# Attention on one Trainium2 core: output stores held back for nine pairs of quads instead of seven, in twelve buffers instead of ten, and a wait ahead of the last nine

## The chip, the cores and the metric

The kernel runs on one core of one Trainium2 chip. The metric is the device time of one execution in microseconds; the median of seven runs is compared. The engines of the core are named as the profile names them: PE is TensorE's matmuls and PEld its weight loads, DVE is VectorE, ACT is ScalarE, POOL is GpSimd, SP is SyncE. A DMA is issued from the queue of an engine, here SP's (listed as q1) or ACT's (q10), and is carried out by the 16 DMA engines that all queues share.

## The reference

Softmax attention without a mask, for 16 x 32 = 512 heads, each with 192 queries, 1024 keys and a head size of 128, all bfloat16:

```
B, H, Sq, Sk, D = 16, 32, 192, 1024, 128

def reference(q, k, v):
    scale = q.shape[-1] ** -0.5
    scores = jnp.einsum("bhqd,bhkd->bhqk", q, k) * scale
    p = _softmax(scores, axis=-1)
    return jnp.einsum("bhqk,bhkd->bhqd", p, v)
```

The inputs are normal numbers times 0.05. Per head, 0.27 MB of keys, as much of values and 0.05 MB of queries come in, and 0.05 MB of output goes out.

## The kernel before

**Quads, fills and pairs.** Four heads make a quad; there are NQ = 128 quads. The work of a quad is cut into three fills, so there are NF = 384 fills, numbered f. For a fill, PE computes scores (`qk`, line 655), ACT takes the exponential from PSUM to SBUF (lines 861 and 864), and PE multiplies with the values (`pv`, line 678) LAG = 4 fills later. The values carry a column of ones, so the same matmuls give the sums of the softmax; DVE takes their reciprocals and scales the result into an output buffer `ob` (`onorm`, line 777, with the reciprocal in line 784 and the scaling in line 788). PE runs `qk` and `pv` of six fills as the body of a loop (line 715), and the last fill and the last four `pv` as straight code behind it. Two quads make a pair; one store writes a pair, 384 KB.

**Ahead of the matmuls.** SP loads keys, queries and values of a quad (lines 558, 543 and 567) into five buffers each. DVE turns the keys (line 763) and queries (line 772), POOL puts the keys in order (line 620) and spreads the values (line 629). A load waits until its buffer is free: the keys until DVE has turned those of five quads ago, the values until `pv` has used those of five quads ago.

**Stores.** `stores` (line 452) lists 65 of them: 63 pairs, and the last two quads one by one. Store i takes buffer i modulo NSO, with NSO = 10, from `ob`. A store in the list `store_at` (line 539) is issued from ACT's queue, behind the exponentials of fill 3(x + c) + 6 + 6 HOLD, where x is its first quad and c the number of its quads. HOLD = 7 puts the store of the first pair behind fill 54, and one store follows every six fills. Only those that come out at fill 372 or before are in the list: 54 of them, numbers 0 to 53. The other eleven are issued by SP in the order of the list, behind its last load (line 596). Each waits until DVE has passed its quads (semaphore s_rc); the store of the last quad is two DMAs of 96 KB, each with a wait for its own `onorm` (s_fin). A DMA-issuing instruction of SP also stays as long as its queue takes no more.

**Buffers that come free.** `onorm` of a pair's first fill waits until the store that used the same buffer NSO pairs ago has landed (line 787).

**The end.** The `pv` of fills 380 to 382 write to the PSUM of scores, so that of fill 380 waits for the exponential before last, and that of fill 381 for the last exponential and the last spread values (lines 683 to 689). DVE then looks over all reciprocals and writes one number, `redo`, which says whether a general version of the kernel has to run; with these inputs it doesn't. Each engine reads `redo` behind a barrier, jumps over the general version and meets the others at a last barrier. SP waits there for all stores to land (`stored`, line 598).

Of the kernel before, what the change touches and what calls it, by code (L numbers as in the profile page):

```python
# [421 lines left out]
def _attention_kernel(nc, q, k, v, out):  # L422
# [9 lines left out]
    NF = 3 * NQ  # L432
    LAG = 4

    PRE = 1
# [3 lines left out]
    NKN, NVS, NKT, NVP = 5, 5, 2, 2  # L439
    GQ = 2  # L440

    NSO, HOLD = 10, 7

    HELD = 2
    VB = 136
# [9 lines left out]
    with ExitStack() as outer:  # L455
        redo = outer.enter_context(nc.sbuf_tensor("redo", [1, 1], mybir.dt.int32))

        def sem(name):
            return outer.enter_context(nc.semaphore(name))
# [13 lines left out]
        s_qk = sem("f_qk")  # L473
# [11 lines left out]
        with ExitStack() as es:  # L485
# [34 lines left out]
            def store(e, i):  # L520
                so = i % NSO
                x, c = stores[i]
                if x + c == NQ:

                    for y in range(2):
                        e.wait_ge(s_fin, y + 1)
                        e.dma_start(
                            of[4 * x + 2 * y:4 * x + 2 * y + 2].rearrange("x (p j) d -> (x p) (j d)", j=3),
                            ob[:, so, 3 * y:3 * y + 3, :].rearrange("p j d -> p (j d)"),
                        ).then_inc(s_st[so], 16)  # L530
                    return
                e.wait_ge(s_rc, 3 * (x + c) + 1)
                e.dma_start(
                    of[4 * x:4 * x + 4 * c].rearrange("(a x) (p j) d -> (x p) a (j d)", x=2, j=3),
                    ob[:, so, 0:6 * c, :].rearrange("p (a j) d -> p a (j d)", j=3),
                ).then_inc(s_st[so], 16)


            store_at = {3 * (x + c) + 6 + 6 * HOLD: i for i, (x, c) in enumerate(stores)
                        if 3 * (x + c) + 6 + 6 * HOLD <= NF - 12}  # L540

            def load_q(e, x):
                e.dma_start(
                    qn[:, x % NKN, :],
                    qf[4 * x:4 * x + 4].rearrange("a (j u) d -> (a j) (u d)", u=6).bitcast(U32),
                ).then_inc(s_qn[x % NKN], 16)
# [3 lines left out]
            def hint(eng):  # L550
                hints[eng.engine] = eng.mark_branch_hint_location()

            @block.sync
            def _(e):
                def load_k(x, lo=0, hi=32):
                    if x >= NKN:
                        e.wait_ge(s_kx, 3 * (x - NKN) + 3)
                    e.dma_start(
                        kn[:, x % NKN, 64 * lo:64 * hi],
                        kf[4 * x:4 * x + 4].rearrange("a (j r) d -> (a j) r d", r=32)[:, lo:hi, :]  # L560
                        .rearrange("p r d -> p (r d)").bitcast(U32),
                    ).then_inc(s_kn[x % NKN], 16)

                def load_v(x, lo=0, hi=4):
                    if x >= NVS:
                        e.wait_ge(s_pv, 3 * (x - NVS) + 2 + BLANK)
                    e.dma_start(
                        vs[:, x % NVS, lo:hi, :],
                        vf[4 * x + lo:4 * x + hi].rearrange("a (m t) d -> m a (t d)", t=T),
                    ).then_inc(s_v[x % NVS], 16)  # L570


                load_k(0)
                e.wait_ge(s_blank, 1)
                load_k(1)
                load_q(e, 1)
                load_v(0, 0, 2)
                e.wait_ge(s_qk, PRE + 1)
                load_v(0, 2, 4)
                load_k(2, 0, 16)  # L580
                e.wait_ge(s_pv, BLANK - 2)
                load_k(2, 16, 32)
                load_q(e, 2)
                for n in range(3, NKN):
                    load_v(n - 2)
                    load_k(n)
                    load_q(e, n)
                for n in range(NQ):
                    if n == NQ // 2:
                        hint(e)  # L590
                    if n + NKN - 2 < NQ:
                        load_v(n + NKN - 2)
                    if n + NKN < NQ:
                        load_k(n + NKN)
                        load_q(e, n + NKN)
                for i in range(len(store_at), len(stores)):
                    store(e, i)
            def stored(e):
                for so in range(NSO):
                    last = (len(stores) - 1) % NSO == so  # L600
                    e.wait_ge(s_st[so], 16 * (len(range(so, len(stores), NSO)) + last))
# [269 lines left out]
def bass_standalone__mha_softmax__near_ridge_kernel(  # L871
    nc: bass.Bass,
    q: bass.AP,
    k: bass.AP,
    v: bass.AP,
    out: bass.AP,
):
    _attention_kernel(nc, q, k, v, out)
# [28 lines left out]
```

## Time and profile before

| | us |
|---|---|
| Median of 7 runs | 815.38 (814.43 to 817.21) |
| The profiled execution, as timed | 816.05 |
| Its span, from the first to the last instruction | 814.3 |
| PE idle in the span | 14.1 |
| Median time of one fill on PE, `qk` and `pv` | 2.054 |
| Last score fill starts | 801.13 |
| Last `pv` ends | 808.9 |
| Last store issued | 809.6 |
| Last of DVE's work (`redo`) | 810.5 |

PE's instructions are busy for 98% of the span, ACT's for 92%, DVE's for 74% and POOL's for 68%. The core reads 293.60 MB and writes 25.17 MB. In the DMA rows, the share is the busy time of the 16 engines together; a share of 1.0 or a little more is full.

Three kinds of lines come below. A row of windows gives, for a stretch of time, its length and then for each engine the busy time with the number of instructions, then the clock that was granted to TensorE, the DMA share and the GB/s. A row of waits gives who waited for what, the total in us, how often, and the longest. A row of the chain of waits, or of the timeline, begins with the start in us and the length in us; in the timeline, the square bracket tells how long the engine was idle before, and what ended it.

### The profile page before, as it was taken

The page shows a single profiled execution, that of the slowest core. Times are in us where ns is not written, and L with a number is a line of the kernel's source. Part 1 is how long each engine was busy: PE and PEld are TensorE (multiplying, and loading weights), DVE is VectorE, ACT ScalarE, POOL GpSimd, SP SyncE. Part 2 cuts the span into 40 slices and gives each one's busy share as a digit, 9 for nine tenths or more (in the row PEclk, how much of TensorE's full clock was granted, in tenths as well). Part 3 has the DMA queues.
Part 4 walks back from the last instruction along what each step waited for, and adds up shares of the span by engine and source line. Part 5 has one row for each costly group of instructions (what it writes and reads, how often), then busy time and mean ns, then how long its engine had stood idle before and what let it go on. Part 6 is the DMA issues. An engine that isn't in the chain of part 4 may idle for free. (4 is left out here: it accounts for less than half of the span.)

```text
span 814.3 us, 71452 instructions
## 1 busy us (share of the span) xinstructions
PE 800.2 (98%) x32996; PEld 714.1 (88%) x32996; DVE 600.7 (74%) x1293; ACT 749.9 (92%) x772; POOL 552.2 (68%) x648
## 2 busy tenths in 40 slices
PE   7999999999999999999999999999999999999996
PEld 6888888888888888888888888888888888888885
DVE  4777777777777777777777777777777777778773
ACT  6899999999999999999999999999999999998994
POOL 5676676676677677667667667766676676766772
PEclk9999999999999999999999999999999999999999
DMA  7999999999999999999999999999999999999995
GB/s 259 405 397 403 399 401 403 409 404 405 409 404 406 408 405 405 407 405 405 408 405 405 407 405 405 405 404 398 398 378 396 402 405 406 381 409 404 385 367 167
DMA packets 138474, 319.20 MB, mean 392 GB/s; under 512 B 7232, under 2 KB 56384, under 8 KB 122176
## 3 DMA queue, kind: packets, MB, share of 16 engines
q1 hardware_dynamic: 109776, 297.36, 93.7%
q10 hardware_dynamic: 28656, 21.43, 7.8%
q14 instruction: 35, 0.29, 0.1%
q8 instruction: 7, 0.11, 0.1%
HBM read 293.60 MB, written 25.17 MB: 391 GB/s over the span
## 5 line engine op out<-in xcount | busy, mean ns | idle before, releaser
L864 ACT ACTIVATE f_pt<-f_s 128x1536 bf16<-128x1536 f32 x384 | 554.5, 1444 | 0.1
L699 PE MATMUL f_o<-f_vp,f_pt 128*64 128x129 bf16 x12368 | 425.4, 222 | 2.0 <-PEq L653 1.8
L670 PE MATMUL f_s<-f_qt,f_kt 32*128 32x192 bf16 (+1 forms) x20528 | 422.7, 226 | 4.2 <-PEq L653 3.4
L620 POOL COPY f_kt<-f_kx 128x768 uint32<-128x768 uint32 (+1 forms) x384 | 300.4, 789 | 185.4 <-DVE f_kx L763 184.4
L699 PEld LDWEIGHTS f_o<-f_vp,f_pt 128*64 128x64 bf16 x12368 | 362.3, 110 | 51.0 <-issue 24.2
L670 PEld LDWEIGHTS f_s<-f_qt,f_kt 32*128 32x128 bf16 x20528 | 348.8, 92 | 40.8 <-issue 5.4
L763 DVE STREAM_TRANSPOSE f_kx<-f_kn 128x768 uint32<-128x768 uint32 (+1 forms) x384 | 334.3, 871 | 27.0 <-DMA f_kn<-in_k_dram 23.6
L629 POOL COPY f_vp<-f_vs 128x1024 uint32<-128x1024 uint32 x256 | 259.9, 1045 | 63.1 <-DMA f_vs<-in_v_dram 62.3
L861 ACT ACTIVATE f_pt<-f_s 128x512 bf16<-128x512 f32 x384 | 229.3, 597 | 52.9 <-PE f_s L670 10.0
L784 DVE RECIPROCAL f_rinv<-f_o 128x2 f32<-128x2 f32 x381 | 64.5, 169 | 165.4 <-PE f_o L699 164.9
L788 DVE TENSOR_TENSOR f_ob<-f_o,f_rinv 128x256 bf16<-128x256 f32 x381 | 161.8, 425 | 13.0
L772 DVE STREAM_TRANSPOSE f_qt<-f_qn 128x384 uint32<-128x384 uint32 x128 | 72.9, 570 | 0.0
L699 PE MATMUL f_s<-f_vp,f_pt 128*64 128x129 bf16 x96 | 3.3, 220 | 1.6 <-issue 1.5
L699 PEld LDWEIGHTS f_s<-f_vp,f_pt 128*64 128x64 bf16 x96 | 2.9, 110 | 1.9 <-issue 1.7
L848 ACT ACTIVATE f_pt<-f_ones 128x1536 f32<-128x1536 bf16 x3 | 4.2, 1472 | 0.0
L608 POOL MEMSET f_vp<- 128x1088 uint32 (+1 forms) x3 | 3.8, 1311 | 0.0
L784 DVE RECIPROCAL f_rinv<-f_s 128x2 f32<-128x2 f32 x3 | 0.5, 170 | 2.6 <-PE f_s L699 2.6
L848 ACT ACT_TABLE_LOAD x1 | 1.3, 1283 | 1.2 <-PEq L892 1.2
L712 PE MATMUL f_o<-f_ones 128*128 128x512 bf16 x2 | 1.0, 622 | 1.1 <-POOL f_ones L605 1.1
L736 DVE MEMSET f_pt<- 128x256 uint32 x4 | 1.1, 272 | 0.9 <-PEq L892 0.9
L729 PE MATMUL f_o<-f_bad,f_ones 128*1 128x1 bf16 x1 | 0.2, 164 | 1.4 <-DVEq L837 1.4
L788 DVE TENSOR_TENSOR f_ob<-f_s,f_rinv 128x256 bf16<-128x256 f32 x3 | 1.3, 424 | 0.3 <-DVE f_rinv L784 0.3
(15 smaller groups left out, 5.6 us busy)
## 6 DMA issues: line engine op xcount, KB each, us to landing
f_kn<-in_k_dram SPq DMA_DIRECT2D x127, 1024.0 KB, 18.0
f_vs<-in_v_dram SPq DMA_DIRECT2D x127, 1024.0 KB, 16.2
f_qn<-in_q_dram SPq DMA_DIRECT2D x127, 192.0 KB, 14.2
out_dram<-f_ob ACTq DMA_DIRECT2D x54, 384.0 KB, 9.5
out_dram<-f_ob SPq DMA_DIRECT2D x9, 384.0 KB, 7.2
f_vs<-in_v_dram SPq DMA_DIRECT2D x2, 512.0 KB, 5.8
f_kn<-in_k_dram SPq DMA_DIRECT2D x2, 512.0 KB, 5.1
f_qn<-in_q_dram ACTq DMA_DIRECT2D x1, 192.0 KB, 5.7
```

The source lines that it names most:

```text
L608: return gp.memset(part.bitcast(U32), 0x3F803F80)
L620: gp.tensor_copy(kt[:, x % NKT].bitcast(U32).rearrange("p U (j s u) c -> p U j s (u c)", s=2, u=2)[:, lo:hi], kx[:, x % 2].rearrange("p (U ...
L629: gp.tensor_copy(vp[:, x % NVP, 2 * T * i: 2 * T * i + 2 * T, 0:D].bitcast(U32), vs[:, x % NVS, 2 * i: 2 * i + 2, :].rearrange("p a (t d) ...
L670: ins = pe.matmul(S[:, c0: c0 + n1 - n0], kt[r, x % NKT, 2 * t + h, :, c], qt[r, x % R, h, n0:n1, c], start=w == 0 and g == 0, stop=w == 3 ...
L699: ins = pe.matmul(O[64 * z: 64 * z + 64, u, 0:129], pt[:, x % R, 2 * y + z, t * SQ + 64 * j: t * SQ + 64 * j + 64], vp[:, x % NVP, (2 * y ...
L763: dve.transpose(kx[:, x % 2].rearrange("p (U s j u) -> p s u U j", s=2, j=32, u=2)[:, :, :, lo:hi], kn[:, x % NKN].rearrange("p (s u U i) ...
L772: dve.transpose(qt[:, x % R].bitcast(U32).rearrange("p b (y j u) c -> p u y b (j c)", y=3, u=2), qn[:, x % NKN].rearrange("p (u y b i) -> ...
L784: dve.reciprocal(ri, O[:, :, 128]).then_inc(s_rc, 1)
L788: ins = dve.tensor_tensor(ob[:, so, 6 * a + 2 * w: 6 * a + 2 * w + 2, :], O[:, :, 0:128], ri.unsqueeze(2).to_broadcast([128, 2, D]), ALU.mult,
L848: return act.activation(part.bitcast(F32), ones[:, 0:1].to_broadcast([128, 2 * T * SQ // 2]), ACT_FN.Copy)
L861: act.activation(pt[:, x % R, 0, c], s1_ps[:], ACT_FN.Exp, scale=scale).then_inc(s_e1, 1)
L864: act.activation(pt[:, x % R, 1:4, c], s3_ps[f % 2][:], ACT_FN.Exp, scale=scale).then_inc(s_e3, 1)
```

## The change

NSO goes from 10 to 12 and HOLD from 7 to 9. The first store then stands behind fill 66, and 52 stores (numbers 0 to 51) are in ACT's list, so SP issues thirteen behind its last load. It issues four of them, numbers 52 to 55; ahead of the fifth, number 56, it waits until all 385 score fills are counted (s_qk of NF + PRE, where PRE = 1 counts one blank fill at the start). `ob` grows by two buffers of 3 KB in each partition, and `stored` waits for twelve semaphores instead of ten.

```diff
@@ -439,7 +439,7 @@
     NKN, NVS, NKT, NVP = 5, 5, 2, 2
     GQ = 2
 
-    NSO, HOLD = 10, 7
+    NSO, HOLD = 12, 9
 
     HELD = 2
     VB = 136
@@ -594,6 +594,9 @@
                         load_k(n + NKN)
                         load_q(e, n + NKN)
                 for i in range(len(store_at), len(stores)):
+
+                    if i == len(store_at) + 4:
+                        e.wait_ge(s_qk, NF + PRE)
                     store(e, i)
             def stored(e):
                 for so in range(NSO):
```

## The prediction

> **What bounds the kernel now.** I read the busy times first, then windows of 40 us, the waits, and the last 15 us piece by piece.
>
> ```profile
> PE 800.2 (98%) x32996; PEld 714.1 (88%) x32996; DVE 600.7 (74%) x1293; ACT 749.9 (92%) x772; POOL 552.2 (68%) x648
> ```
>
> PE is busy nearly throughout, so only its 14.1 us of idle time can be won, and what lies behind its end. The windows tell where the idle time is:
>
> ```profile
> 80.00:120.00 40.00, 40.00 (x1673) 35.80 (x1671) 29.93 (x66) 37.81 (x40) 27.15 (x33) 1.00 1.04 400
> 200.00:240.00 40.00, 40.00 (x1678) 35.73 (x1668) 30.40 (x66) 37.71 (x40) 28.48 (x34) 1.00 1.04 404
> 640.00:680.00 40.00, 40.00 (x1652) 35.84 (x1648) 30.61 (x65) 37.70 (x41) 28.92 (x34) 1.00 1.04 407
> 680.00:720.00 40.00, 39.51 (x1642) 35.13 (x1637) 29.38 (x64) 36.93 (x39) 26.48 (x31) 1.00 1.03 394
> 720.00:760.00 40.00, 39.16 (x1622) 34.91 (x1622) 32.05 (x67) 36.80 (x39) 28.08 (x32) 1.00 1.03 396
> ```
>
> PE has no gap until 680 us and loses 0.49 and 0.84 us in the two rows after. By the starts of the score fills the loss is larger: those between 684 and 766 us stand 2.03 us further apart, in sum, than at the 2.054 us per fill of all others. The DMA share is 1.03 or 1.04 in every row, before the first store (125.1 us) as well as behind it: the DMA engines are always full. The waits say who is late:
>
> ```profile
> POOL f_vp L629 <- DMA f_vs<-in_v_dram: 12.8, 12, 2.1
> ...
> POOL f_vp L629 <- DMA f_vs<-in_v_dram: 16.2, 9, 2.2
> ```
>
> ```profile
> 745.92 2.03 POOL L629 COPY f_vp<-f_vs 128x1024 uint32<-128x1024 uint32 x2 [2.21 <-DMA f_vs<-in_v_dram]
> ...
> 749.71 0.52 PE L670 MATMUL f_s<-f_qt,f_kt 32*128 32x64 bf16 x22 [0.72 <-PEq L653]
> ```
>
> These are the windows 540 to 640 and 640 to 690 us; from 140 to 540 us POOL never waits for values. At 745.92 the spreading starts 2.21 us late, the ordering of keys behind it on POOL is late too, and PE stands still for 0.72 us. So the loads have a lead that they lose. By the landing records, values land 0.7 us ahead of their spreading in quad 8 (63.8 and 64.5 us), 4.15 us in quad 16 (109.6 and 113.8), 4.6 us in quad 26 (170.8 and 175.4) and 0.05 us from quad 90 (569.6) on. One of the 16 engines drops behind the others: keys of quad 16 land between 98.8 and 100.7 us, of quad 96 between 588.2 and 597.0. The lead is its lead.
>
> The last stretch is another matter:
>
> ```profile
> 802.27 0.60 ACT f_pt L861
> 802.87 1.35 ACTq L485
> 804.22 0.04 issue
> 804.26 0.24 PE f_s L699
> 804.50 1.52 issue
> 806.02 1.97 PE f_s L699 x63
> ```
>
> ```profile
> 802.00:803.00 1.00, 1.00 (x42) 0.85 (x32) 0.00 (x0) 0.89 (x3) 0.00 (x0) 1.00 1.03 319
> 803.00:804.00 1.00, 1.00 (x42) 0.99 (x36) 0.60 (x2) 1.00 (x1) 0.00 (x0) 1.00 1.06 333
> 804.00:805.00 1.00, 0.40 (x7) 0.11 (x2) 0.59 (x2) 0.21 (x1) 0.00 (x0) 1.00 0.69 217
> 805.00:806.00 1.00, 0.00 (x0) 0.00 (x0) 0.00 (x0) 0.00 (x0) 0.00 (x0) 1.00 0.14 45
> ```
>
> Behind the last exponential PE loads two sets of weights and stops for 1.52 us with no semaphore to wait for. The DMA list shows what comes in meanwhile: one packet of the queue of instructions that feeds PE,
>
> ```profile
> q8 instruction: 1, 0.02, 11.8%
> ```
>
> at 803.58 us, for 0.95 us. Such packets are seen only in the first 25 us and behind PE's loop. Until 804.3 us the engines are full of SP's stores (319 to 333 GB/s).
>
> **The change part by part.** *Two stores leave the stretch before the last load.* With HOLD = 9, 52 instead of 54 stores are issued from ACT's queue ahead of it; they start 12 fills, 24.6 us, later. What two stores cost the loads has three prices. By bytes at 404 GB/s: 2 x 393,216 B / 404 GB/s = 1.95 us. By the lead: it grew 0.435 us a quad without stores (quads 8 to 16: 3.48 us / 8) and 0.05 with them (quads 20 to 26), 0.77 us for a store of two quads, 1.54 for two. The third is what is left if the loads couldn't use the stretch without stores, being held by full buffers: then the loss only starts 24.6 us later, and 2.03 us over 122 us (from 684 - 16 to 790) is 1.66%, 0.41 us. Against the third speaks the share of 1.04 before 125 us. PE's loss is what the last loads are late, so it shrinks by as much, to at least 0: I take 1.75 us, the middle of the first two, with 0.41 and 2.03 as ends. The last score fill ends at 802.25 - 1.75 = 800.50.
>
> *Four stores behind the last load, then the wait.* In the stretch around 800 us there is no store traffic but of those four, on the engine that is behind. So the instruction packet can start earlier. The next one, at 807.11 with the engines idle (share 0.08), started 1.09 us after PE had gone on at 806.02. The stall of 1.52 us is worth between 0 and 1.52 us; a packet that meets the stores' burst could make it longer. I take 1.52, as the stores are the only other traffic.
>
> Here the page "Runtime: NRT & Kernel Launch" of the Trainium skill, section "Instruction fetch mechanics", speaks against the price: instructions come in blocks of 16 KiB while the block before runs, and the cost of crossing into the next one is mostly hidden. The 1.52 us above are not hidden; by the rule the term would be 0.
>
> *Nine stores behind the wait.* SP is free when the last score fill is counted, as ACT is at 802.27, now 800.52. Queued behind the wait on SP are seven stores of 384 KB, one of 192 KB and the two halves. How fast do they go?
>
> ```profile
> L533 SPq DMA_DIRECT2D out_dram<-f_ob x4: 829/1076/1203, 798.0 to 801.4; - x4
> ...
> DMA to landing us min/median/max: 5.7/6.0/6.2
> ```
>
> ```profile
> L527 SPq DMA_DIRECT2D out_dram<-f_ob x2: 344/344/345, 808.7 to 809.6; - x2
> ```
>
> With the engines full of stores alone they move 320 GB/s (799 to 803 us), 1.23 us for 384 KB. The last half, issued at 809.60, had its first packet at 810.44, 0.84 later, its last at 810.84 and landed at 811.23, 0.39 later. So: 800.52 + 0.84 + 8 x 1.23 (the small ones make one more) + 0.39 = 811.59. From the landing SP needs 0.7 us: its other waits and its drain, 0.35 (812.38 to 812.91 for all of them before, most of it still to come), then the barrier, 814.0 to 814.3. End: 812.3.
>
> *The other way to the end*, by PE, DVE, the barrier and ACT's jump, was 814.3; less 1.75 and 1.52 it is 811.05. ACT's jump took from 812.18 to 814.02 in a quiet stretch; now the stores run until 811.2. If its instructions come only behind them, ACT is ready 1.67 us later (814.02 less 812.35, the first packet for the jump), at 812.9, and the end is 813.2. I take the stores' 812.3, between these.
>
> *At no cost:* two more issues on SP, 0.37 us each, under stores that are in flight; the two less on ACT (0.38 us each) beside 52.9 us of its idle time ahead of line 861. Larger `ob` moves nothing else. A buffer is stored 11 fills before it is written again, as before, 22.6 us; the longest landing was 18.1. The last quad's buffer is that of store 52, which lands around 797, some 7 us ahead. The waits in `stored` cost 0.07 us.
>
> **The sum:** 812.3 - 814.3 = -2.0 us. It is made against the span; the profiled execution took 816.05 as timed, 0.67 over the median. The difference goes to the median: 815.38 - 2.0 = 813.4.
>
> **The rivals.** *R1, the loads gain 0.41 only.* For it: 24.6 us of earlier traffic are far from 684 us. Against: a full DMA there. Then the last store lands at 812.9, the end is 813.6, -0.7, median 814.7.
>
> *R2, the closing jump or the packet for PE waits behind the burst.* For it: nine stores in flight just where all engines jump. End 813.2 to 813.5, or -1.0, median 814.4.
>
> On this, "DMA: Bandwidth & Descriptors", section "Queues, rings and completion order", says that each engine turns to the next queue after a packet of at most 64 descriptors. At 33 to 39 ns per store descriptor in this trace that is an estimate of 2.5 us at worst. No run here separates it.
>
> *R3, slower: SP can't fill the engines.* Between 789.5 and 798 us an issue took up to 2.45 us, with engines idle in between. If the seven stores of the burst go at 2.37 us (the mean of the three longest), SP is done issuing them at 817.1, with the last three (1.05), the landing (1.29 from the end of an issue) and 0.7 at 820.2: +5.9, median 821.2. It makes the kernel slower by over 0.2% from 1.77 us per store on. Against it: those issues waited for the engine that was behind with loads; at 798 us and later, without loads, it was 0.83 to 1.20 us.
>
> **How the numbers follow.** A measurement of this kernel can tell about 0.2%, 1.63 us, from no change: faster begins at 813.75. The forecast has 0.64; its own range is 811.8 (the loss gone altogether and 1.06 us per store, as the engine that is behind did them between 797.75 and 804) to 813.9, with 0.58 under 813.75 and 0.06 within. R1 has 0.11, all within. R2 has 0.13: 0.09 within, 0.04 faster, where the loss is gone altogether. R3 has 0.12, slower. Together 0.62, 0.26 and 0.12. The range, 812.1 to 815.8, leaves R3 out above and 0.05 below.
>
> **What would show it.** POOL's waits for values begin some 20 quads later; PE's gaps between 680 and 770 us are under 0.5 us; the last score fill ends near 800.5. The stall behind the last exponential is under 0.3 us. From 801.4 to 811.2 us the DMA share is full at 320 GB/s, and SP's store waits are the last thing before the closing barrier. The prediction is wrong if the gaps of 680 to 770 us stay at 1.6 us or more, or if the issues behind the wait take over 1.8 us each.

## The result, and the profile after

The changed kernel takes 815.97 us (median of 26 executions, 814.52 to 819.36), against 814.11 us of the kernel before (63 executions, 811.87 to 817.21). The ratio is 1.0027 with a 95% interval of 1.0019 to 1.0035: it is 0.27% slower, where 0.25% faster was forecast. The profiled execution of the changed kernel took 815.61 us, near its median; that of the kernel before took 816.05, 1.9 us over the larger sample's median.

First the late loads. These are the windows of the changed kernel, with the columns of before (length, then PE, PEld, DVE, ACT, POOL, clock, DMA share, GB/s):

```profile
640.00:680.00 40.00, 40.00 (x1671) 35.78 (x1668) 29.92 (x66) 37.80 (x40) 27.02 (x32) 1.00 1.04 403
680.00:720.00 40.00, 40.00 (x1680) 35.72 (x1666) 30.30 (x66) 37.70 (x40) 28.17 (x34) 1.00 1.03 389
720.00:760.00 40.00, 39.44 (x1630) 35.20 (x1627) 32.03 (x67) 37.04 (x39) 27.16 (x32) 1.00 1.03 397
```

The gap of 0.49 us in the middle row is gone, and in the last 0.56 us are left of 0.84. (What is left there stays without late loads too, as is shown further down.) POOL's waits for values from 540 to 640 us are gone, and from 640 to 690 us there is one:

```profile
POOL f_vp L632 <- DMA f_vs<-in_v_dram: 0.4, 1, 0.4
```

By the landing records the values' lead comes down to 0.05 us at quad 109 (686.7 us), 20 quads later than before (quad 89, 563.9 us). The last score fill starts at 799.46 us, not at 801.13. Then the last stretch, as the chain of waits (start in us, length, what):

```profile
800.61 0.60 ACT f_pt L864
801.20 1.35 ACTq L485
802.55 0.04 issue
802.60 0.24 PE f_s L702
802.84 0.37 issue
803.21 1.97 PE f_s L702 x63
```

The stall behind the last exponential is 0.37 us instead of 1.52. PE's last `pv` ends at 806.09, 2.8 us sooner than before, and DVE's last work at 807.87:

```profile
807.72 0.15 DVE L842 CAST redo<-f_o 1x1 int32<-1x1 f32 x1 [0.34 <-PE f_o L733]
```

Yet the span ends at 813.9, only 0.4 us sooner. The timeline of SP's queue says what is still going on, and so does the list of its issues (shortest, median and longest in ns):

```profile
800.60 7.88 SPq L533 DMA_DIRECT2D out_dram<-f_ob  x8
808.52 1.88 SPq L527 DMA_DIRECT2D out_dram<-f_ob  x2
```

```profile
L533 SPq DMA_DIRECT2D out_dram<-f_ob x8: 372/1086/1371, 800.6 to 807.4; - x8
```

SP issues stores from 800.60 until 810.40, without a pause. Ahead of the closing barrier each engine runs one last instruction, its drain. DVE's drain starts at 808.31 us, 0.45 us behind its last work; SP's starts at 810.45, 0.06 us behind its last issue and 2.1 us behind DVE's. All engines pass that barrier at 810.73. ACT's jump over the general version lasts until 813.56, and the last store lands at 812.43, so that SP is through its waits for the stores at 812.86, ahead of ACT.

### The profile page after: what moved, and what is told of

It reads as the page before. It is cut to its first block, busy times and chain, and to the rows that moved or that the text cites. A ratio compares the mean times of both kernels' runs of the same rounds, so it can differ in the third digit from the quotient of the medians.

```text
span 813.9 us, 71452 instructions
## 1 busy us (share of the span) xinstructions
PE 799.4 (98%) x32996; PEld 713.3 (88%) x32996; DVE 599.1 (74%) x1293; ACT 749.8 (92%) x772; POOL 551.4 (68%) x648
```

## The experiments

Two measures are used. One is the stretch from the start of the last score fill to the end of the span, in the one profile of each kernel. It leaves out whatever the loads did before. The other is the time, in two forms: the ratio to executions of the kernel before on the same chip, and the difference of means, with intervals by resampling. The means are compared with 116 executions of the kernel before, those that were timed with the experiments: their mean is 814.76 us and their standard deviation 1.46, so that a dozen executions leave about 0.9 us open on either side. The 63 executions that were timed with the result are not among them. Their mean is 814.12, 0.64 us lower (0.25 to 1.03). So one series of executions differs from another by more than chance within a series explains, and against all 179 every difference of means below would be 0.23 us higher.

**e1, e8: the kernel before, unchanged.** One execution differs from the next by several us; how much of the loss to late loads is usual?

> The kernel before, unchanged, to see how one execution of it differs from the next. Theory A (the profiled execution of before was a usual one: PE's gaps of 2.0 us between 680 and 770 us, a stall of 1.5 us behind the last exponential): this profile shows both within 0.5 us, and the last score fill ends near 802. Theory B (it was an unusual one, and most executions of before lose less to late loads): the last score fill ends 1 to 3 us earlier, near 800, with gaps under 1 us. By both the ratio to before is 1.000 within 0.15%.

> The kernel before once more, for a third profile of it. The two so far lost 1.75 and 3.5 us to late loads behind 40 us and took 816.05 and 817.14 us, both far above their median. If a usual execution loses less, this profile, when its time is near 814.3, shows a loss near 1 us and a last score fill that starts before 800; if it loses as much, the difference lies elsewhere, in the first 40 us (7.0 to 7.3 us lost there in both).

The ratios were 0.9997 (0.9984 to 1.0011) and 1.0001 (0.9983 to 1.0020). The two profiles took 817.14 and 814.84 us. By the starts of the score fills, compared with 2.054 us per fill, they lost 3.5 and 0.83 us from the 40th fill on; the first profile had lost 1.75 by the same count. So the loss is not a constant: in the execution near the median it is half of what the prediction was to save. But that execution had lost 1 us more than the other two in the first 40 fills (8.3 against 7.3 and 7.0), and its last score fill started at 801.18, not before 800. That extra loss doesn't explain the smaller one later: in quad 16 its values had the lead of the first profile (4.19 and 4.15 us). Neither theory A nor B came out clean.

The third profile gave something else, a test of the stall that nobody had planned. In it hardly a store was under way when the last score fill started, on about one of the 16 engines:

```profile
801.00:802.00 1.00, 1.00 (x54) 0.91 (x52) 0.60 (x2) 1.00 (x1) 0.35 (x1) 1.00 0.07 24
```

```profile
804.31 0.24 PE f_s L699
804.55 0.37 issue
804.92 1.97 PE f_s L699 x63
```

With a DMA share of 0.07 the same kernel stalls for 0.37 us, not 1.52 (or 1.19 in e1, with the engines full). The stretch was 13.19 us in the first profile, 12.79 in e1 and 11.93 here.

**e2: the changed kernel, unchanged.**

> The changed kernel, unchanged. Both theories: ratio near 1.0027; SP's last issue ends about 9.8 us behind the last score fill (eight stores' worth at 1.23 us) and the barrier behind it comes with it, while DVE is done some 2 us before. Nothing here separates A from B but the spread of the times.

The ratio was 1.0035 (1.0021 to 1.0048). SP's last issue ended 10.88 us behind the start of the last score fill (10.94 in the first profile), that is 9.7 us behind its end, and the stretch was 14.30 us (14.41).

**e3: the delay alone.**

```diff
-    NSO, HOLD = 10, 7
+    NSO, HOLD = 12, 9
```

> Twelve buffers and nine pairs of delay, without the wait: SP issues all thirteen stores behind its last load. Theory A: the gaps between 680 and 770 us shrink from 2.0 to about 0.8 us or less, the stores end as in before, and the time is 1.2 to 2.0 us below before (ratio 0.9975 to 0.9985). Theory B: in most executions there is little to win, ratio 0.999 to 1.000. If instead two more stores behind the last load are what costs, the last store is issued 2 us later and the ratio is 1.001 to 1.002.

The ratio was 0.9997 (0.9984 to 1.0010), by means -0.64 us (-1.52 to +0.19). SP issued thirteen stores behind its last load and was done with the last at 807.6, before DVE (808.35), so two more stores there cost SP nothing. But the engines were full of them when PE needed its instructions:

```profile
801.00:802.00 1.00, 1.00 (x40) 0.93 (x34) 0.59 (x2) 1.00 (x1) 0.00 (x0) 1.00 1.05 335
```

```profile
802.21 0.24 PE f_s L700
802.45 1.25 issue
803.69 1.97 PE f_s L700 x63
```

The stall is 1.25 us and the stretch 13.27 us, close to the 13.19 of the first profile of before.

**e4: the wait alone.**

```diff
                 for i in range(len(store_at), len(stores)):
+
+                    if i == len(store_at) + 4:
+                        e.wait_ge(s_qk, NF + PRE)
                     store(e, i)
```

> Ten buffers and seven pairs of delay as before, with the wait ahead of the fifth of SP's eleven stores: seven stores, six stores' worth of data, come behind the last score fill. If the burst behind the wait is what holds the end in the changed kernel: it takes 6 x 1.23 = 7.4 us here instead of 9.8, SP's last issue comes 2.4 us nearer to the last score fill, about level with DVE's last work. Theory A: the stall of 1.5 us is gone, 1.2 us below before, ratio 0.9985. Theory B: within 0.1% of before, or up to 0.1% above.

The ratio was 0.9996 (0.9979 to 1.0013), by means -0.08 us (-1.14 to +1.12). The profiled execution was the slowest of its twelve (4.6 us of PE's time lost in one gap at 25.6 us), but its stretch can be read: 12.05 us, with no stall of over 0.15 us, SP done with its issues at 813.2 and at its drain 0.05 us before DVE. With seven stores behind it, the wait does in the stretch what it was forecast to do; the times show no gain.

**e9, four ahead, e10, e5, e12, e11, e6: how many stores stand ahead of the wait.** All are the changed kernel but for one number:

```diff
-                    if i == len(store_at) + 4:
+                    if i == len(store_at) + 6:
```

with 2, 5, 6, 6, 7 and 9 in turn.

e9, two ahead:

> Two stores ahead of the wait, so ten stores' worth of data behind it. If the amount of data behind the wait sets the end, the stretch from the start of the last score fill to the end is 1.14 us (the fill) + 10 x 1.23 + 3.47 (barrier and closing jump, from the changed kernel) = 16.9 us, 2.5 us more than in the changed kernel, and the ratio to before is 1.005 to 1.006. Rival (the wait costs by being there, or elsewhere, not by its amount): ratio 1.002 to 1.003.

e10, five ahead:

> Five stores ahead of the wait, seven stores' worth behind it. Amount: 1.14 + 7 x 1.23 + 3.47 = 13.2 us for the stretch, ratio between those of four and six ahead: 0.9985 to 1.001. Rival as above: 1.002 to 1.003.

e5, six ahead:

> The changed kernel with six stores ahead of the wait instead of four, so that seven stores, six stores' worth of data, are left behind it. Theory T (SP's issues behind the wait hold the barrier): from the last score fill SP needs 7.4 us to issue them instead of 9.8, its drain comes level with DVE's, and the stretch from the start of the last score fill to the end falls from 14.3 to about 12.1 us, as with the wait alone. Time 1.5 to 2.3 us below the changed kernel: ratio to before 0.999 to 1.0005. Rival L (the landing of the last stores holds the end, not their issue): 12.4 to 13 us. Rival S (the tail isn't what costs): no change, ratio 1.002 to 1.003.

e12, six ahead again:

> Six stores ahead of the wait once more, to see whether 0.9976 of before holds: 0.997 to 0.999. If it was luck of eleven runs: 0.999 to 1.001.

e11, seven ahead:

> Seven stores ahead of the wait, five stores' worth behind it. Amount: SP needs 6.2 us, less than PE and DVE to their end, so that the stretch stays at the 12.1 us that DVE's end sets, as with six ahead; ratio 0.997 to 0.999. If the stores ahead come so late that they fill the engines when PE's instructions are fetched, the stall behind the last exponential is back (up to 1.3 us) and the ratio is 0.9985 to 1.0005.

e6, nine ahead:

> The changed kernel with nine stores ahead of the wait: four are left, three stores' worth of data. Theory T: SP no longer holds anything; the stretch is 12.1 us if PE's instructions still come early, and up to 13.3 us if the five additional stores still fill the engines when the last score fill starts, which the stall behind the last exponential will show (0 against 1.2 us). Ratio to before 0.998 to 1.000. Rival S: ratio 1.002 to 1.003.

| ahead of the wait | stores' worth behind it | SP's last issue ends, us from the start of the last score fill | stretch, us | ratio to before | difference of means, us |
|---|---|---|---|---|---|
| 2 (e9) | 10 | 13.4 | 17.14 | 1.0063 (1.0045 to 1.0081) | +4.84 (3.82 to 5.82) |
| 4 (the change, e2) | 8 | 10.9 | 14.41, 14.30 | 1.0027, 1.0035 | +1.71 (1.19 to 2.23) |
| 5 (e10) | 7 | 9.7 | 13.12 | 1.0014 (1.0001 to 1.0027) | +0.89 (0.19 to 1.66) |
| 6 (e5, e12) | 6 | 8.5 | 12.23, 12.43 | 0.9976 (0.9961 to 0.9991), 1.0000 (0.9986 to 1.0013) | -0.68 (-1.26 to -0.10) |
| 7 (e11) | 5 | 7.7 | 12.06 | 0.9999 (0.9984 to 1.0015) | -0.68 (-1.57 to +0.29) |
| 9 (e6) | 3 | 7.2 | 11.56 | 0.9997 (0.9979 to 1.0014) | -0.27 (-1.33 to +0.89) |

From seven stores' worth on, each further one costs 1.2 to 1.4 us of the stretch, and the numbers expected (13.2 and 16.9) were met within 0.25 us. With six or fewer, DVE's drain is the last one ahead of the barrier, 8.35 to 8.90 us behind the start of the last score fill (in e5 SP's drain comes 0.11 us sooner than DVE's, in the changed kernel 2.1 us later), and less to store brings little more. The times follow in the same order, with 3.1 us between two and four ahead and 2.4 between four and six. Six ahead takes 2.4 us off the changed kernel. Whether it also beats the kernel before isn't settled: e5 says so, e12 does not, and the two together only against the 116 executions, not against all 179 (-0.45 us, -1.00 to +0.10). SP with two ahead, and with six:

```profile
803.31 10.39 SPq L533 DMA_DIRECT2D out_dram<-f_ob  x10
813.75 1.86 SPq L527 DMA_DIRECT2D out_dram<-f_ob  x2
```

```profile
800.07 5.41 SPq L533 DMA_DIRECT2D out_dram<-f_ob  x6
805.52 1.87 SPq L527 DMA_DIRECT2D out_dram<-f_ob  x2
```

In e9 SP is still issuing at 815.6 with DVE done at 810.6; in e5 it ends at 807.4, with DVE done at 807.1 and 0.45 us from its drain.

**e7: the same burst from two queues.** Is it the issuing or the data?

```diff
-                    store(e, i)
+                    if not len(store_at) + 4 <= i < len(store_at) + 8:
+                        store(e, i)
...
                     if f in store_at:
                         store(act, store_at[f])
+                for i in range(len(store_at) + 4, len(store_at) + 8):
+                    store(act, i)
```

> The changed kernel, with four of the nine held stores (numbers 56 to 59) issued from ACT's queue behind its last exponential, the other five from SP behind the wait: the same data at about the same time, but SP has half the issues. Theory T: SP's last issue comes about 4 us sooner, DVE's end decides the barrier, and the stretch falls from 14.3 to 12.5 to 13.3 us, bounded by the landing of the stores about 11.9 us behind the last score fill's start plus 0.7. Rival L: the landing decides already in the changed kernel, so nothing changes: 14.3 us, ratio 1.0027.

The ratio was 1.0025 (1.0011 to 1.0038), by means +1.91 us (1.29 to 2.60), and the stretch 14.84 us: nothing was won. SP was done at 807.0, at its drain 0.4 us before DVE, and the closing barrier passed at 807.7: 2.5 us sooner than in the changed kernel, counted from the start of the last score fill. But the engines were full until 811:

```profile
800.04 4.39 SPq L533 DMA_DIRECT2D out_dram<-f_ob  x4
805.09 1.95 SPq L527 DMA_DIRECT2D out_dram<-f_ob  x2
```

```profile
809.00:810.00 1.00, 0.00 (x0) 0.00 (x0) 0.00 (x0) 0.00 (x0) 0.00 (x0) 0.52 1.04 326
810.00:811.00 1.00, 0.00 (x0) 0.00 (x0) 0.00 (x0) 0.00 (x0) 0.00 (x0) 0.50 0.97 297
```

The last store landed at 813.15, SP went to its last drain at 813.52, and the span ended at 813.74. The part of the expectation that put the end at 0.7 us behind the landing held (0.59); the landing itself came 14.25 us behind the start of the fill, not 11.9, and 1.3 us later than in the changed kernel (12.97); why the same data landed later from two queues, no run shows. So the theory that the issues alone hold the end falls. Eight stores' worth behind the last score fill are too much in two ways that lie within 1 us of each other. One is the issue: SP's issues of 384 KB took 0.37 us with nothing in flight and up to 1.37 us behind that: 9.8 us for eight stores' worth, the 1.22 us apiece at which the stores land. The other is the landing: in the changed kernel it let SP through its waits 0.7 us before ACT had jumped.

## Why the prediction was wrong

**The failed step: what is behind the wait on SP, and who waits for that.** The prediction left SP's issues out of the way to the closing barrier. It counted two more issues on SP at no cost, "under stores that are in flight", and let the end come 0.7 us behind the last landing, or by PE, DVE and the barrier 3.27 us sooner than before. But SP itself has to come to that barrier, and with the engines full its issues took 0.57 to 1.37 us each instead of 0.37. From the end of the last score fill to the end of the span it had 11.8 us (800.50 to 812.3); measured were 13.27 (800.60 to 813.87). The rows that would have told were in its own fences: four stores, issued from 798.0 to 801.4 at 0.83 to 1.20 us each, are the pace at which a full queue takes them, and eight stores' worth at 1.23 us end 9.8 us behind the fill, where DVE is done after 7.3 (807.87). The table above shows it: take stores away from behind the wait, and the stretch shrinks by what they take, until DVE's end decides. e7 adds that the landing would have held the end at nearly the same place: 0.7 us from the landing was right there, but the last landing came 0.8 us later than worked out even in the changed kernel (812.43 for 811.59), as the last of the 16 engines was later than the first (811.65), and 1.2 us behind the last data (811.92) in e7. Last of all was ACT's jump, at 813.56. Of the prediction's own signs of being wrong neither came: the gaps of 680 to 770 us were 0.7 us, and no issue took over 1.37 us. It failed where it had named no sign.

**The loads: the mechanism held, the term was too large.** The last score fill was to end at 800.50; it ended at 800.60, and the lead lasted 20 quads longer, for "some 20". The delay does build a lead. Five profiles have the same lead of 4.15 to 4.20 us in quad 16; in quad 26 it is 4.58 and 5.44 us in the two with seven pairs of delay, and 6.38 to 6.93 in the three with nine. But the end met was luck in part: 0.45 of the 1.67 us by which the last score fill came sooner are from the first 40 fills, ahead of the first store in both kernels.

The term itself counted something that stays when no load is late. Of the 1.75 us that the first profile of before lost behind its 40th fill, 0.98 went in the six fills 356 to 361. There DVE looks over the reciprocals of the first 351 fills in three pieces, 2.6 us in all, ahead of its turning of queries and keys. The same six fills lose 0.76 to 1.20 us in all fourteen profiles: 1.05 in e8, the kernel before without late values, and 1.18 in e6, where values land 3.5 us or more ahead of their spreading. These are lines of e6:

```profile
747.54 1.07 DVE L810 TENSOR_SCALAR f_chk<-f_rinv 128x702 f32<-128x702 f32 x1
748.64 0.58 DVE L775 STREAM_TRANSPOSE f_qt<-f_qn 128x384 uint32<-128x384 uint32 x1
...
749.67 0.92 PE L673 MATMUL f_s<-f_qt,f_kt 32*128 32x192 bf16 x36 [0.67 <-PEq L656]
749.87 0.63 POOL L623 COPY f_kt<-f_kx 128x512 uint32<-128x512 uint32 x1 [1.65 <-DVE f_kx L766]
```

PE stands still for 0.67 us until the turned queries are there, and POOL, in that stretch, waits for DVE's turned keys and never for values. In the first profile of before, values were late as well, and the gap of 0.72 us at 749.71 ends with POOL's ordering of keys, as the prediction read it (that piece took 1.52 us beside DVE's look, for 0.86 in e6). But loads in time don't win these fills back, so the loss could not shrink to 0. That is read from the traces; no run left DVE's look out. Outside these six fills ten of the profiles show -0.2 us (2.054 is a little more than a fill takes), the first profile 0.8, e1 2.6, e11 0.3 and e12 1.6. Beyond that common part, late loads thus cost 1.0, 2.8, 0 and 0 us in the four profiles with seven pairs (the three of before, and e4). With nine pairs it is 0.5 us in e11, 1.8 in e12 and nothing in the other eight: 0.7 us less in the mean, from few profiles. The delay alone brought -0.64 us (-1.52 to +0.19) in time, for a term of -1.75. And e12, with nine pairs, lost more in these two windows than the first profile of before with seven:

```profile
680.00:720.00 40.00, 39.01 (x1624) 34.77 (x1622) 29.13 (x64) 36.40 (x39) 26.44 (x31) 1.00 1.03 388
720.00:760.00 40.00, 39.07 (x1619) 34.81 (x1615) 32.15 (x68) 36.68 (x39) 28.14 (x32) 1.00 1.04 397
```

So the true size isn't settled to better than that, and what the prediction took for the loss of the kernel was partly that of one execution, which took 1.9 us over the median.

**The stall: right in kind, sized by one execution.** 1.52 us were to go, and 1.15 went (from 1.52 to 0.37, where "under 0.3" was to show it). But the three profiles of before have 1.52, 1.19 and 0.37 us, so a usual execution had less to give. The stall is long where stores fill the engines from the start of the last score fill on (1.52, 1.19, 1.25 us in the first profile, e1 and e3), and at most 0.42 us in the other eleven profiles. The packet for PE starts 2.1 to 2.5 us behind the start of the fill in the first group, and 0.9 us in the changed kernel, e2, e5 and e8. The latest of the eleven is e11, where the engines were full for the first 1.1 us: the packet starts 1.5 us behind, and the stall is 0.42. The Trainium skill's page "Runtime: NRT & Kernel Launch", section "Instruction fetch mechanics", says that the cost of crossing into the next block is mostly hidden. That fits here where the DMA engines are idle (0.42 us and less), and not where stores fill them.

**The rivals.** R1 was right in kind, in that the loads gain less than 1.75 us in time, but its sum had the wrong end too. R2 didn't happen: ACT's jump took 1.88 us (811.69 to 813.56) while the last stores landed, and 1.84 before. R3 named the right engine and the wrong mechanism: SP filled the DMA engines, at 1.22 us per store by the landings, as forecast, far from the 1.77 that was to decide; being done with issuing was late all the same. The chance of 0.12 for slower stood on that rival alone.

**The sum.** In the profile the end came at 813.87 for 812.3, and 1.47 of these 1.57 us are the tail. By the profiles the stretch grew from 12.64 us (mean of three of before) to 14.36 (two of the change), +1.7 us. The mean of the times grew by 1.71 us against the 116 executions, and by 2.21 (1.65 to 2.81) for the 26 and 63 that were timed together. That leaves nothing to be seen of a gain by the loads. Against the delay alone the wait costs 1.1 us in the stretch and 2.4 in the means, which is 1.3 more; the spread of a dozen executions could make that, and it stays open.

## What to carry to other kernels

Work that is held back to the end is paid there at the pace of what it is held for: divide it by that pace and compare with what the last engine still has to do; here 7.7 us from the end of the last score fill to DVE's drain covered six stores of 1.23 us, and neither seven nor eight. An issuing engine that has to meet the others at a barrier comes there behind its last issue, so its issues belong into the sum as well as the last landing. And before a loss is put into a sum, look whether the profiled execution is a usual one, and whether all of its gaps go when the cause does that the longest wait suggests: here its time stood 1.9 us over the median, as much as the gain that was read from it, and over half of the loss stays when no load is late.

## What the runs showed of the hardware

Where stores filled the DMA engines (share 1.00 to 1.05 for 2.5 us from the start of the last score fill), the packet of PE's instructions started 2.1 to 2.5 us behind that start instead of 0.9 to 1.5, and PE stood still for 1.19 to 1.52 us instead of 0.42 or less where its straight code begins. In every profile there is a load whose last engine lands 9.6 to 11.0 us behind its first. SP's issue of a store of 384 KB took 0.37 us with nothing in flight and up to 1.37 us with the engines full of stores. In the fourteen profiles PE lost 5.9 to 11.8 us in the first 40 fills, over half of it in gaps that began in the first 30 us; where PE's gap at 25 us grew to 2.9 (e6) and 4.6 us (e4), the granted clock was 0.5 for 6.8 us behind it.
